# Moving low parts of weights and of g to GpSimd in the first tiles, under a new written order of all engines

## The chip, the cores and the metric

One core of a Trainium2 chip runs the whole program: TensorE (PE) multiplies, VectorE (DVE), ScalarE (ACT) and GpSimd (POOL) do the elementwise work, and SyncE (SP) issues every transfer between HBM and SBUF. The metric is the device time of one execution in microseconds, the median of several runs. Before the change it was 848.84 us in three runs (847.57 to 848.84).

## The reference

A sliding-window attention (window 64, 8 batches of 8 heads, 576 tokens, head size 64) is followed by a feed-forward layer on the 4608 x 512 result:

```python
scores = scale * np.matmul(q, k.transpose(0, 1, 3, 2))
mask = (rel >= 0) & (rel < window)           # rel = query position - key position
attn = exp(scores - max) / (sum + 1e-09)     # masked scores are -1e9
x = matmul(attn, v)                          # then tokens x (heads * head size)
h = x @ w_in                                 # 512 -> 2048
g = np.maximum(h, 0.0) ** 2
out = g @ w_out                              # 2048 -> 512
```

All inputs and outputs are float32.

## The kernel before, in words

**Tiles.** The 4608 tokens are 12 tiles of 384. Attention is done in sections of four pairs (a block of 64 queries, a group of heads), three sections to a tile: sections 0 to 2 make x of tile 0, 3 to 5 that of tile 1, 6 to 8 that of tile 2. The hidden size 2048 is 16 slices of 128, so a tile takes 16 steps, each a first product (12 matmuls, line 404) and a second one (9 matmuls, line 446).

**High and low parts.** A float32 operand of a product is split into a rounded high part and the rest, the low part; each product is made of three (high by high, high by low, low by high). The low part is one subtraction: line 132 for a weight slice (128 x 1024), line 423 for g (128 x 384), line 315 for x. A weight arrives as raw words and is first put together by two `tensor_scalar` (lines 120 and 121) and two `scalar_tensor_tensor` (lines 123 and 125) on VectorE, after ScalarE made its magnitude (line 118); ScalarE then writes the high part (line 129). Only two such weights can be under way, because the tile `a` has two halves. g is the square (line 416 on ScalarE, 418 otherwise) of the positive part (line 413).

**The order.** The work up to the first two steps of tile 2 stands in a string of tokens in the order in which each engine is to take its own: a letter, a number, and where there is a choice a last letter for the engine (d VectorE, a ScalarE, p GpSimd). The tokens that matter here:

| token | work | engine before |
|---|---|---|
| L, N, v, w, q, B | loads of q and k for tiles 0 and 1, of v, of a weight slice, of q and k of a later batch; a store of a finished slice | SP queue |
| T, U / t, u | transposes of q and k / their copies out of PSUM | PE / DVE or ACT |
| S, o, s, z, y, e f, k, R, m | scores of a section; copy, mask, maximum, scale, exponentials, sum, reciprocal, division | PE, ACT, DVE, DVE, POOL, ACT, POOL, DVE, POOL |
| X x V H Q | transposed weights, masking, product with v; high and low part of x | PE, DVE, PE, ACT, DVE |
| a b c d h l | the weight slice: lines 118, 120 and 121, 123, 125, 129, 132 | ACT, DVE, DVE, DVE, ACT, DVE |
| M, O | first and second product of a step | PE |
| r p g G | positive part, square, high part, low part of g | ACT, ACT (8 of 34 on DVE), ACT, DVE |
| D, Z, W, K | turn of a later batch, output copy, output store, matmuls with no result | DVE, ACT, SP, PE |

Each engine and the SP queue take their tokens strictly in this order; an instruction that waits holds all behind it. M0 to M4 are tile 0 with slices 0 to 4, M5 to M9 tile 1 with the same slices, then tile 1 runs ahead of tile 0 with slices 5 to 15: M22 is the first step that uses slice 15, the last one to be prepared. Behind the string a planner (lines 640 to 708) orders all later work; it is the same before and after.

**What VectorE does up to M22.** Through l15: the preparation of 16 weight slices (b, c, d, l), 21 low parts of g, one division, 5 copies, and of each of six sections the mask, maximum, reciprocal, x and Q; one H and two turns. GpSimd has only y, k and m of the sections up to there.

Of the kernel before, what the change touches and what calls it, by code (L numbers as in the profile page):

```python
# [8 lines left out]
F32 = mybir.dt.float32  # L9
# [3 lines left out]
ALU = mybir.AluOpType  # L13
# [16 lines left out]
def window_attention_relu2_ffn(ctx: ExitStack, tc: tile.TileContext, q, k, v, w_in, w_out, out):  # L30
# [74 lines left out]
        sp.dma_start(raw[:, 1], wo_v[:, f, :])  # L105


    def weight(op, f):
        if op == "a":
            wa[f] = a_t[:, f % 2].bitcast(I32)  # L110
        a = wa[f]
        if op in "acd":
            words = wraw[f].rearrange("p n (e w) -> p w (n e)", w=2)
            lower, upper = words[:, 0, :], words[:, 1, :]
        else:
            av = a.bitcast(F32).rearrange("p (n e) -> p n e", n=2)
        if op == "a":
            act.activation(a.bitcast(F32), upper.bitcast(F32), AF.Abs, scale=2.0 ** -80)
        elif op == "b":
            dve.tensor_scalar(a.bitcast(F32), a.bitcast(F32), 1.875 * 2.0 ** -64, 2.0 ** -95, ALU.min, ALU.max)  # L120
            dve.tensor_scalar(a, a, 4, 1, ALU.logical_shift_left, ALU.logical_shift_right)
        elif op == "c":
            dve.scalar_tensor_tensor(a, lower, 29, a, ALU.logical_shift_right, ALU.bitwise_or)  # L123
        elif op == "d":
            dve.scalar_tensor_tensor(a, upper, -0x80000000, a, ALU.bitwise_and, ALU.bitwise_or)  # L125
            wraw.pop(f)
        elif op == "h":
            wparts[f] = wpool.tile([P, 2, 2, DM], F32R, name="w")
            act.copy(wparts[f][:, :, 0], av)
        else:  # L130
            w = wparts[f]
            dve.tensor_tensor(w[:, :, 1], av, w[:, :, 0].bitcast(F32), ALU.subtract)  # L132
# [277 lines left out]
    def evac(op, n, eng=None):  # L410
        if op == "r":
            rg[n] = r_t[:, n % 2]
            act.activation(by_half(rg[n]), ordered(hs.pop(n)), AF.Relu)  # L413
        elif op == "p":
            if eng == "a":
                act.activation(rg[n], rg[n], AF.Square)
            else:
                dve.tensor_tensor(rg[n], rg[n], rg[n], ALU.mult)
        elif op == "g":
            gs[n] = (ghi_t[:, n % 3], glo_t[:, n % 2])  # L420
            act.copy(gs[n][0], rg[n])  # L421
        else:
            dve.tensor_tensor(gs[n][1], rg.pop(n), gs[n][0].bitcast(F32), ALU.subtract)  # L423

# [11 lines left out]
    hs, rg, gs = {}, {}, {}  # L436
# [43 lines left out]
    while n1 < NF:  # L480
# [18 lines left out]
        b12 O13 r14 p14a d11 g14 B4 M15 G14 h11 c12 O14 r15 l11 p15a g15 d12 a13 B5 M16 G15 h12 b13 O15 r16 l12
        p16a g16 c13 a14 B6 M17 G16 b14 O16 r17 p17a d13 g17 B7 M18 G17 h13 c14 O17 r18 l13 p18a g18 d14 a15 B8  # L500
        M19 G18 h14 b15 O18 r19 l14 p19a g19 c15 B9 M20 G19 D0 O19 r20 p20a d15 q2 g20 M21 G20 h15 D1 O20 r21
        l15 p21a g21 q3 G21 M22 O21 r22 p22d g22 G22 M23 D2 O22 r23 p23d q4 g23 M24 G23 Z22 W22 O23 r24 p24d g24
        G24 S6 M25 o6a D3 q5 s6 O24 r25 z6 p25a y6 g25 f6 G25 S7 O25 e6 o7d s7 v9 k6 z7 M26 R6 y7 m6p f7 D4 X6
# [42 lines left out]
    with tc.manual_schedule(engines={E.PE, E.DVE, E.Activation, E.Pool, E.SP}):  # L546
        for token in order.split():
            op, eng = token[0], token[-1] if token[-1] in "dap" else None
            n = int(token[1:].rstrip("dap"))
            if op in "LN":  # L550
                load_first("LN".index(op), n)
            elif op == "v":
                load_v(*divmod(n, (NB + 1) // 2))
            elif op == "w":
                fetch_w(n)
            elif op == "q":
                load_qk(1 + n // NPAIR, n % NPAIR)
            elif op == "D":
                turn(1 + n // NPAIR, n % NPAIR)
            elif op in "TU":  # L560
                ps_f[op, n] = turn_first("TU".index(op), *divmod(n, 2))
            elif op in "tu":
                copy_first("tu".index(op), *divmod(n, 2), ps_f[op.upper(), n], copier(eng))
            elif op == "K":
                idle(n)
            elif op in "abcdhl":
                weight(op, n)
            elif op == "M":
                hs[n] = mm1(*steps[n], lambda kk, part, f=steps[n][1]: wparts[f][:, 0, part, kk * P:(kk + 1) * P])
            elif op in "rpgG":  # L570
                evac(op, n, eng)
            elif op == "B":
                keep(n)
            elif op in "ACEF":
                mix(op, n)
            elif op == "O":
                mm2(*steps[n], *gs.pop(n), lambda part, f=steps[n][1]: wparts[f][:, 1, part])
            elif op in "ZW":
                for tb in range(NTB):
                    put(op, steps[n][0], tb)  # L580
            else:
                section(op, n, eng)
# [513 lines left out]
```

## Time and profile before

| what | value |
|---|---|
| median of 3 runs | 848.84 us (847.57 to 848.84) |
| profiled execution | 847.38 us, its span 845.1 us |
| PE busy | 829.0 us, 98% |
| DVE busy | 590.5 us, 70% |
| ACT busy | 407.3 us, 48% |
| POOL busy | 184.9 us, 22% |
| mean granted PE clock | 0.998 |

The span runs from the first instruction to the last; the rest of the execution's time, 2.3 us, lies around it. The page's busy shares are means over stages with different limits. The page also shows the span in 40 slices of 21 us: in the first seven, DVE is at 5, 8, 9, 9, 9, 9 and 6 tenths, and POOL at 1, 2, 2, 0, 0, 0 and 3 tenths, while PE is at 7 tenths in the first slice, 8 in the second and 9 or more from the third on.

### The profile page before, as it was taken

How to read it: one execution, taken by the hardware profiler on the slowest of the kernel's cores; microseconds unless marked ns; L12 is line 12 of the kernel's file. 1: busy time of each engine (PE TensorE's matmuls, PEld its weight loads, DVE VectorE, ACT ScalarE, POOL GpSimd, SP SyncE). 2: the span in 40 equal slices, each digit the busy share in tenths (PEclk: the TensorE clock that was granted, in tenths of full speed). 3: DMA queues.
4: the chain of work that ended last, by engine and by line, in shares of the span. 5: the costliest groups of instructions: out<-in, count | busy, mean ns of one | idle time of the engine just before them, and what ended most of it. 6: DMA issues, size and time to landing. Idle time of an engine off the chain costs nothing.

```text
span 845.1 us, 17706 instructions
## 1 busy us (share of the span) xinstructions
PE 829.0 (98%) x6754; PEld 761.2 (90%) x6754; DVE 590.5 (70%) x889; ACT 407.3 (48%) x1127; POOL 184.9 (22%) x239
## 2 busy tenths in 40 slices
PE   7899999999999999999999999999999999999998
PEld 5788989899999999999999999999999999999997
DVE  5899996746767866767687765788755668544553
ACT  5887874646446555544442354453454424222221
POOL 1220003204557420311320121141112132010110
PEclk9999999999999999999999999999999999999999
DMA  9989956584688875999896797999785556686411
GB/s 230 231 257 346 306 239 130 86 171 126 153 210 251 214 170 119 305 245 238 169 319 225 179 217 161 285 224 271 212 237 157 188 194 182 236 259 212 136 66 74
DMA packets 273012, 173.92 MB, mean 206 GB/s; under 512 B 190497, under 2 KB 239649, under 8 KB 270881
## 3 DMA queue, kind: packets, MB, share of 16 engines
q1 hardware_dynamic: 272928, 172.80, 73.8%
q8 instruction: 53, 0.87, 0.5%
q14 instruction: 31, 0.25, 0.1%
HBM read 138.15 MB, written 34.60 MB: 204 GB/s over the span
## 4 chain that ended last, share of the span: by engine, by line
PE 86%; SPq 5%; DVE 3%; DMA 3%; issue 2%; ACT 1%; POOL 0%; DVEq 0%; ACTq 0%; POOLq 0%
PE banks L993 29%; PE banks L912 26%; PE banks L446 11%; PE banks L404 11%; PE banks L235 3%; PE banks L298 3%; DMA w<-in_moe_w_out_dram 2%; PE banks L276 2%; SPq L147 1%; SPq L185 1%; SPq L157 1%; DVE a L123 1%; DVE a L125 1%; SPq L104 1%; DVE g L423 1%
## 5 line engine op out<-in xcount | busy, mean ns | idle before, releaser
L993 PE MATMUL banks<-w 128*128 128x512 f32 x1152 | 257.5, 380 | 0.0
L993 PEld LDWEIGHTS banks<-w 128*128 128x128 f32 x1152 | 215.7, 189 | 28.4
L404 PE MATMUL banks<-x,w 128*128 128x384 f32 x768 | 137.1, 328 | 1.9 <-ACT r L413 1.4
L446 PE MATMUL banks<-w,g 128*128 128x512 f32 x576 | 136.1, 382 | 0.2
L404 PEld LDWEIGHTS banks<-x,w 128*128 128x128 f32 x768 | 126.6, 189 | 6.1 <-ACT r L413 3.3
L912 PE MATMUL banks<-x,w 128*128 128x384 f32 x768 | 130.3, 326 | 0.0
L938 POOL TENSOR_TENSOR g<-g 128x384 f32<-128x384 f32 x64 | 59.5, 934 | 323.1 <-ACT g L949 308.2
L912 PEld LDWEIGHTS banks<-x,w 128*128 128x128 f32 x768 | 125.6, 189 | 0.0
L446 PEld LDWEIGHTS banks<-w,g 128*128 128x128 f32 x576 | 106.2, 189 | 14.4 <-DVE g L423 1.2
L263 ACT ACTIVATE sel<-sel,nm 128x64 f32<-128x64 f32 x272 | 90.8, 336 | 25.9 <-DVE nm L257 22.8
L912 PE MATMUL banks<-w 128*128 128x384 f32 x576 | 100.7, 329 | 0.0
L1001 DVE TENSOR_TENSOR w<-w,banks 128x512 f32<-128x512 f32 x72 | 49.5, 687 | 69.9 <-PE banks L993 69.9
L912 PEld LDWEIGHTS banks<-w 128*128 128x128 f32 x576 | 93.8, 189 | 1.9
L983 ACT CAST w<-w 128x512 fp32r<-128x512 f32 x48 | 29.8, 620 | 72.9 <-PE banks L993 72.9
L413 ACT ACTIVATE r<-banks 128x384 f32<-128x384 f32 x64 | 31.5, 492 | 66.8 <-PE banks L404 64.6
L983 ACT CAST w<-g 128x512 fp32r<-128x512 f32 x48 | 29.7, 621 | 62.2 <-PE banks L993 58.2
L272 POOL TENSOR_TENSOR sel<-sel,nm 128x512 f32<-128x512 f32 x33 | 36.1, 1095 | 107.3 <-ACT g L949 51.7
L263 ACT ACTIVATION_READ_ACCUMULATOR sel<-sel,nm 128x1 f32 x272 | 51.2, 188 | 0.0
L423 DVE TENSOR_TENSOR g<-r,g 128x384 fp32r<-128x384 f32 x64 | 37.6, 588 | 18.0 <-ACT g L421 9.7
L535 POOL TENSOR_TENSOR a<-w 128x256 f32<-128x256 f32 x28 | 24.9, 906 | 105.3 <-DVE w L132 79.6
L280 DVE TENSOR_TENSOR pt<-banks,masks 128x1024 f32<-128x1024 f32 x33 | 40.3, 1220 | 10.9 <-PE banks L276 10.9
L926 DVE TENSOR_TENSOR w<-banks,r 128x384 f32<-128x384 f32 x64 | 38.5, 601 | 13.3 <-PE banks L912 13.0
(103 smaller groups left out, 990.0 us busy)
## 6 DMA issues: line engine op xcount, KB each, us to landing
w<-mixed SPq DMA_DIRECT2D x128, 256.0 KB, 5.1
w<-kept SPq DMA_DIRECT2D x64, 512.0 KB, 7.2
w<-kept SPq DMA_DIRECT2D x96, 256.0 KB, 5.9
kept<-w SPq DMA_DIRECT2D x16, 1024.0 KB, 7.5
vt<-in_v_dram SPq DMA_DIRECT2D x144, 64.0 KB, 2.9
w<-in_moe_w_in_dram SPq DMA_DIRECT2D x16, 512.0 KB, 7.5
w<-in_moe_w_out_dram SPq DMA_DIRECT2D x16, 512.0 KB, 8.4
raw<-in_q_dram SPq DMA_DIRECT2D x112, 72.0 KB, 3.4
```

Of the source, the lines that this page charges most:

```text
L263: act.activation(sels[i][:, w, hd], sels[i][:, w, hd], AF.Exp, bias=nms[i][:, n], scale=SCALE, accum_out=sums[i][:, n])
L272: (dve if eng == "d" else pool).tensor_tensor(p, p, rs[i][:, :, None].broadcast_to([P, SW * 2, QB]), ALU.mult)
L280: dve.tensor_tensor(pts[i].rearrange("p (w n) q -> p w n q", n=2), ps_t[i][:, :, None, :].broadcast_to([P, SW, 2, P]), masks.rearrange("p ...
L404: pe.matmul(h_ps, lhsT=weights(kk, part), rhs=in_turn(x[xx][:, kk // 2, kk % 2]), start=n == 0, stop=n == 3 * NK - 1)
L423: dve.tensor_tensor(gs[n][1], rg.pop(n), gs[n][0].bitcast(F32), ALU.subtract)
L446: pe.matmul(acc(t, tb), lhsT=gg[:, ts], rhs=in_turn(weights(part)), start=f == 0 and n == 0, stop=f == NF - 1 and n == 2)
L912: pe.matmul(ps[:, :TT], lhsT=w[:, part, kk * P:(kk + 1) * P], rhs=in_turn(x[:, xx, kk]), start=n < 4 and m == 0, stop=m == 5, skip_group_c ...
L926: plan("dve", 0.6, lambda: dve.tensor_tensor(to(), ps, other(), ALU.add), [kps, ko], keys, 0, after)
L938: plan("pool", 0.95, lambda: pool.tensor_tensor(x(), x(), x(), ALU.mult), [], keys)
L983: plan("act", 0.62, lambda: act.copy(high(c), src()), g_keys, [kh], 0, freed("hi") if new else [])
L993: pe.matmul(ps, lhsT=gg[:, m // 2, m % 2], rhs=in_turn(wo_slot(w[m])[:, part]), start=m == 0 and n == 0, stop=m == 3 and n == 2)
L1001: plan("dve", 0.72, lambda: dve.tensor_tensor(by_half(parts(tb)), by_half(parts(tb)), ordered(ps), ALU.add), [key], [kp])
```

## The change

Three helper calls can now put their instruction on GpSimd, and the whole string of tokens is written anew, to the second step of tile 2. In the new string

- ten of the sixteen low parts of weights are GpSimd's (l0 to l3, l7, l8, l10 to l13); six stay with VectorE (4, 5, 6, 9, 14, 15);
- 23 of the 34 low parts of g are GpSimd's, 14 of the 34 squares too (16 stay with ScalarE, 4 with VectorE; before 26 and 8);
- of the copies t, VectorE has two and ScalarE eight (before five each); of the first six H, VectorE has three (0, 4, 5; before 5 alone); five y and six k move from GpSimd to VectorE; m0 moves from VectorE to GpSimd, m6 and m7 the other way;
- the loads stand in another order: q0 and q1 (eight transfers each) come early, weights 11, 9, 14 and 15 out of their turn, the stores B are strewn between them.

```diff
-    def weight(op, f):
+    def weight(op, f, eng=None):
...
             w = wparts[f]
-            dve.tensor_tensor(w[:, :, 1], av, w[:, :, 0].bitcast(F32), ALU.subtract)
+            (pool if eng == "p" else dve).tensor_tensor(w[:, :, 1], av, w[:, :, 0].bitcast(F32), ALU.subtract)
...
-                dve.tensor_tensor(rg[n], rg[n], rg[n], ALU.mult)
+                (pool if eng == "p" else dve).tensor_tensor(rg[n], rg[n], rg[n], ALU.mult)
...
-            dve.tensor_tensor(gs[n][1], rg.pop(n), gs[n][0].bitcast(F32), ALU.subtract)
+            (pool if eng == "p" else dve).tensor_tensor(gs[n][1], rg.pop(n), gs[n][0].bitcast(F32), ALU.subtract)
...
     order = """
-        L0 L1 w0 L2 T0 v0 T1 t0a t1d S0 w1 T2 o0a T3 K5 t2d v1 s0 t3d a0 z0 S1 L3 y0 b0 f0 N0 T4 K3 c0 o1a L4
...
-        h7 c8 O8 r9 l7 p9a g9 d8 a9 M10 G9 h8 b9 O9 r10 l8 p10a g10 c9 a10 B0 M11 G10 b10 O10 r11 p11a d9 g11 B1
...
+        L0 T1 T0 t0d L1 w0 t1a K3 S0 L2 o0a s0 z0 y0d T2 t2d T3 t3a w1 K11 S1 a0 L3 v0 b0 c0 f0 o1a s1 z1 y1d T4
+        t4a e0 k0d R0 K2 T5 t5a K4 S2 d0 a1 b1 m0p X0 x0 e1 o2a s2 z2 T6 t6a f1 K2 T7 t7a V0 k1p R1 S3 h0 c1 v1
+        y2p f2 H0d Q0 N0 U0 d1 m1p X1 u0a e2 k2d R2 x1 l0p o3a s3 z3 m2p L4 T8 t8a h1 K7 T9 w2 t9a X2 x2 V1 a2
+        H1a Q1 N1 U2 b2 u2a U1 c2 y3p f3 v2 l1p V2 w3 u1a S4 U3 H2a Q2 d2 e3 k3p R3 o4a s4 z4 y4d a3 m3p b3 w4
+        M0 X3 u3a S5 x3 h2 l2p v5 r0 c3 p0p f4 e4 k4p M1 R4 r1 o5a s5 v3 V3 g0 d3 H3a Q3 p1a g1 M2 a4 z5 G0p O0
+        b4 h3 m4p X4 x4 c4 d4 G1p r2 O1 w5 q0 p2a y5p l3p g2 G2p e5 f5 k5p v4 v6 h4 V4 H4d w6 M3 r3 O2 w8 R5 Q4
...
+        l8p a10 b10 c10 h9 l9d O9 G11p M12 O10 r12 p12p M13 r13 g12 O11 a11 D1 M14 w15 p13a g13 G13p d10 h10
...
-                weight(op, n)
+                weight(op, n, eng)
```

**GpSimd's queue around the first products.** Before, it holds only the sections' small steps up to the division of section 5:

```order
L272 TENSOR_TENSOR sel_79<-sel_79,nm_81 128x512
L266 TENSOR_SCALAR nm_81<-nm_81 128x8
L272 TENSOR_TENSOR w_111<-w_111,nm_81 128x512
L257 TENSOR_SCALAR nm_81<-nm_81 128x8
L266 TENSOR_SCALAR nm_81<-nm_81 128x8
```

Now, from the division of section 1 on:

```order
L272 TENSOR_TENSOR sel_79<-sel_79,nm_81 128x512
L132 TENSOR_TENSOR w_324<-a_84,w_324 128x2x512
L272 TENSOR_TENSOR w_111<-w_111,nm_81 128x512
L257 TENSOR_SCALAR nm_81<-nm_81 128x8
L132 TENSOR_TENSOR w_374<-a_84,w_374 128x2x512
L266 TENSOR_SCALAR nm_81<-nm_81 128x8
L272 TENSOR_TENSOR w_111<-w_111,nm_81 128x512
L132 TENSOR_TENSOR w_550<-a_84,w_550 128x2x512
L418 TENSOR_TENSOR r_82<-r_82 128x384
```

The divisions (line 272) of sections 2 and 3 now stand behind the low parts of weights 0 and 1 (line 132), and behind them come the low part of weight 2 and the first square (line 418).

**VectorE's queue in the middle of the weights** (`a_84` is the tile of two weights, the numbered `w` a raw slice or a finished one, `g_83` and `r_82` the tiles of g). Before, every slice takes its two `tensor_scalar`, lines 123 and 125, and a low part:

```order
L120 TENSOR_SCALAR a_84<-a_84 128x1024
L121 TENSOR_SCALAR a_84<-a_84 128x1024
L132 TENSOR_TENSOR w_1023<-a_84,w_1023 128x2x512
L123 SCALAR_TENSOR_TENSOR a_84<-w_727,a_84 128x1024
L423 TENSOR_TENSOR g_83<-r_82,g_83 128x384
```

Now two slices follow one another with no low part of a weight and one of g:

```order
L123 SCALAR_TENSOR_TENSOR a_84<-w_750,a_84 128x1024
L125 SCALAR_TENSOR_TENSOR a_84<-w_750,a_84 128x1024
L120 TENSOR_SCALAR a_84<-a_84 128x1024
L121 TENSOR_SCALAR a_84<-a_84 128x1024
L123 SCALAR_TENSOR_TENSOR a_84<-w_898,a_84 128x1024
L125 SCALAR_TENSOR_TENSOR a_84<-w_898,a_84 128x1024
L423 TENSOR_TENSOR g_83<-r_82,g_83 128x384
```

**GpSimd's queue at the same place** had nothing between the division of section 5 and the planner's first work; now it has

```order
L132 TENSOR_TENSOR w_949<-a_84,w_949 128x2x512
L423 TENSOR_TENSOR g_83<-r_82,g_83 128x384
L418 TENSOR_TENSOR r_82<-r_82 128x384
L423 TENSOR_TENSOR g_83<-r_82,g_83 128x384
L132 TENSOR_TENSOR w_1010<-a_84,w_1010 128x2x512
L423 TENSOR_TENSOR g_83<-r_82,g_83 128x384
```

These are l7, the low part of g of step 8, the square of step 10, the low part of g of step 9, l8 and the low part of g of step 11.

More of the change, by code (lines that the diff above doesn't have):

```diff
@@ L499, in window_attention_relu2_ffn @@
[L499 to L503, printed above, removed]
@@ new lines, in window_attention_relu2_ffn @@
+        O14 M17 a13 d12 h12 G15d O15 B8 b13 r17 p17a B7 c13 q3 d13 g17 p16p l12p g16 G16d a14 h13 M18 r18 p18a
+        G17p O17 g18 l13p M19 B5 a15 B9 b14 c14 d14 b15 r19 h14 l14d p19p O16 g19 M20 G19d G18p O18 r20 c15 d15
+        p20a g20 h15 M21 l15d O19 r21 M22 p21p q2 D2 G20p O20 r22 p22a g22 M23 g21 G21p r23 B3 O21 p23a g23 B1
+        G22p M24 r24 p24p g24 O22 Z22 M25 G23d r25 O23 M26 v8 D3 G24p O24 q4 r26 S6 p25p o6a s6 M27 v10 g25 z6
+        y6d G25p S7 o7d O25 p26a q5 D5 q7 r27 M28 g26 G26p O26 f6 e6 s7 z7 y7d f7 D4 r28 M29 p27d e7 g27 S8 G27p
```

19 lines of the change are left out of this document (7 added, 12 removed).

## The prediction

> **What bounds the kernel now.** I first read the busy time by stage: the stretch up to the first product, the one up to about M6, the one up to M22, and the rest of the written order. Columns are the stretch, its length, then the busy time of PE, weight loads, DVE, ACT and POOL, the granted clock, the DMA share and GB/s.
>
> ```profile
> 9.80:39.80 30.00, 25.22 (x406) 21.58 (x405) 27.64 (x41) 24.43 (x86) 6.46 (x12) 0.94 0.99 225
> 39.80:66.80 27.00, 25.11 (x263) 21.94 (x261) 26.57 (x33) 21.72 (x57) 4.80 (x6) 1.00 0.89 274
> 66.80:132.00 65.20, 64.95 (x346) 59.99 (x347) 63.63 (x70) 50.22 (x70) 0.01 (x1) 1.00 0.81 278
> 132.00:187.70 55.70, 55.13 (x517) 49.78 (x516) 33.50 (x51) 28.57 (x100) 13.82 (x24) 1.00 0.66 127
> ```
>
> VectorE is busy for 117.8 of the 122.2 us up to M22, and from 66.8 on PE is full too: both run without a gap, so whichever loses time there moves the end. Behind M22 PE is full alone (55.13 of 55.70), and the page shows it at 9 tenths or more in all slices but the first two. What M22 loses or gains therefore arrives at the end of the kernel: nothing later has room to take it back, and at most 0.6 us can be won in the last stretch.
>
> Second, the timelines of VectorE and PE at the borders of these stretches:
>
> ```profile
> 9.86 0.69 DVE L202 COPY qk<-banks 128x512 f32<-128x512 f32 x1 [2.06 <-PE banks L196]
> 12.38 0.68 DVE L120 TENSOR_SCALAR a<-a 128x1024 f32<-128x1024 f32 x1
> ...
> 38.33 0.69 DVE L315 TENSOR_TENSOR x<-banks,x 128x512 fp32r<-128x512 f32 x1
> ...
> 60.17 1.23 DVE L132 TENSOR_TENSOR w<-a,w 128x1024 fp32r<-128x1024 f32 x1
> 61.31 0.69 DVE L315 TENSOR_TENSOR x<-banks,x 128x512 fp32r<-128x512 f32 x1
> ...
> 130.73 1.18 DVE L132 TENSOR_TENSOR w<-a,w 128x1024 fp32r<-128x1024 f32 x1
> ```
>
> ```profile
> 39.85 2.20 PE L404 MATMUL banks<-x,w 128*128 128x384 f32 x12
> ...
> 130.03 2.11 PE L446 MATMUL banks<-w,g 128*128 128x512 f32 x9
> 131.97 2.11 PE L404 MATMUL banks<-x,w 128*128 128x384 f32 x12
> ```
>
> VectorE works from 9.86. Q2 (38.33, line 315) ends at 39.02 and M0 follows at 39.85. The last low part of a weight, l15, ends at 131.91, and M22, the first step with that slice, starts at 131.97. So there is no slack at M22: the time at which VectorE is through its list is the time of M22. An instruction begins 0.09 before the one ahead of it ends (61.31 against 60.17 + 1.23); I take 0.08 off each duration below. A second product is 1.94 (130.03 to 131.97).
>
> **Do the two engines work beside one another?** This decides the case, and the trace has it. Third, timelines of GpSimd and VectorE where both work, with the usual durations (minimum, median, maximum in ns) of two of the lines:
>
> ```profile
> 51.36 1.05 POOL L272 TENSOR_TENSOR sel<-sel,nm 128x512 f32<-128x512 f32 x1 [0.39 <-DVE nm L269]
> 51.69 1.80 DVE L132 TENSOR_TENSOR w<-a,w 128x1024 fp32r<-128x1024 f32 x1
> ...
> 43.13 1.33 DVE L125 SCALAR_TENSOR_TENSOR a<-w,a 128x1024 int32<-128x1024 int32 x1
> 43.27 1.27 POOL L266 TENSOR_SCALAR nm<-nm 128x8 f32<-128x8 f32 x1 [2.95 <-ACT sel L263]
> ...
> 417.89 1.83 POOL L864 TENSOR_TENSOR w<-a 128x768 f32<-128x768 f32 x1 [9.57 <-ACT a L313]
> 418.49 1.25 DVE L257 TENSOR_SCALAR nm<-nm 128x8 f32<-128x8 f32 x1
> ...
> 419.79 1.83 POOL L864 TENSOR_TENSOR w<-a,w 128x768 f32<-128x768 f32 x1
> 420.30 0.56 DVE L926 TENSOR_TENSOR w<-banks,r 128x384 f32<-128x384 f32 x1
> ...
> L132 DVE TENSOR_TENSOR w<-a,w x16: 1181/1218/1803, 18.4 to 130.7; 128x1024 fp32r<-128x1024 f32 x16
> ...
> L266 POOL TENSOR_SCALAR nm<-nm x10: 238/241/1270, 17.0 to 174.3; 128x8 f32<-128x8 f32 x10
> ```
>
> The low part of a weight, usually 1.22, took 1.80 and ended 1.08 after GpSimd's division (51.36 + 1.05 = 52.41): it stood still until GpSimd was through. The other way round, GpSimd's little addition, usually 0.24, took 1.27 and ended at 44.54, just behind VectorE's line 125 (44.46). VectorE's tiny scale at 418.49 ended at 419.74, with GpSimd's subtraction (419.72). But line 926, whose first operand lies in PSUM, ran its 0.56 inside a GpSimd subtraction. So GpSimd and VectorE take turns, for whole instructions, where VectorE works on SBUF alone (lines 120, 121, 123, 125, 132, 418, 423 and the tiny steps); beside its instructions with a PSUM operand GpSimd is free. I count transposes and reductions, too, as free.
>
> **The change, part by part: VectorE's list up to l15.** Groups of the trace up to M22 (busy us, mean ns):
>
> ```profile
> L125 DVE SCALAR_TENSOR_TENSOR a<-w,a 128x1024 int32<-128x1024 int32 x16 | 23.0, 1442 | 0.0
> L123 DVE SCALAR_TENSOR_TENSOR a<-w,a 128x1024 int32<-128x1024 int32 x16 | 22.2, 1392 | 0.0
> L132 DVE TENSOR_TENSOR w<-a,w 128x1024 fp32r<-128x1024 f32 x16 | 20.0, 1253 | 1.1 <-ACT w L129 1.0
> L423 DVE TENSOR_TENSOR g<-r,g 128x384 fp32r<-128x384 f32 x22 | 12.5, 567 | 0.0
> L120 DVE TENSOR_SCALAR a<-a 128x1024 f32<-128x1024 f32 x16 | 11.3, 708 | 1.0 <-ACT a L118 1.0
> L121 DVE TENSOR_SCALAR a<-a 128x1024 int32<-128x1024 int32 x16 | 11.1, 694 | 0.6
> ...
> L202 DVE COPY qk<-banks 128x512 f32<-128x512 f32 x4 | 2.7, 677 | 8.3 <-PE banks L196 8.3
> ```
>
> Removed: ten l of 1.25 - 0.08 = 1.17 (11.7 us), 13 G of 0.49 (6.4), and one division and three copies t, taken at 0.6 each by the copy's row (2.4; one of the copies is shorter). Added: two squares, priced as the low part of the same size (1.0), two H at a copy's price (1.2), five tiny y and k at 0.1 (0.5). Net 17.8 us less: 117.8 becomes 100.0.
>
> Of these 100.0, the lines that take turns with GpSimd are the four weight lines (67.6), six l (7.5), eight G (4.5), two squares (1.1) and the tiny ones (0.8): 81.5, less 0.08 for each of 85 instructions, 74.7. Free are 25.3.
>
> **GpSimd's list up to the same place**, through G18, which O18 before M21 needs. Prices from the whole span (minimum, median, maximum ns):
>
> ```profile
> L539 POOL TENSOR_TENSOR a<-a x56: 446/459/849, 135.0 to 301.6; 128x128 f32<-128x128 f32 x56
> ...
> L864 POOL TENSOR_TENSOR w<-a x3: 1822/1829/1839, 417.9 to 680.4; 128x768 f32<-128x768 f32 x3
> ...
> L938 POOL TENSOR_TENSOR g<-g x64: 824/829/1771, 338.7 to 818.4; 128x384 f32<-128x384 f32 x64
> ...
> L272 POOL TENSOR_TENSOR sel<-sel,nm x33: 1043/1046/1312, 23.6 to 669.0; 128x512 f32<-128x512 f32 x33
> ```
>
> No subtraction of 384 or 1024 columns on GpSimd is in the trace. The line through 128 columns (0.459) and 768 (1.829) gives 2.14 ns a column: 1.01 us for a G, and beyond its end 2.38 for an l (bounds: not under 1.83; in proportion to 768 columns 2.44). Ten l 23.8, twelve G 12.1, nine squares at 0.83 7.5, six divisions at 1.05 6.3, seven y and k at 0.24 1.7: 51.4 us, almost all in turns with VectorE. Each moved instruction holds VectorE up for about twice what it took there (2.38 for 1.25, 1.01 for 0.57).
>
> [...]
>
> **The sum at M22.** Least: every free us of VectorE lies beside GpSimd and nobody waits for anything else. From the first line 120 (12.38, hardly moved): 12.38 + 74.7 + 51.4 = 138.5. Most: none of it overlaps and VectorE's gaps of before (122.2 - 117.8 = 4.4) stay: 9.86 + 100.0 + 4.4 + 51.4 = 165.7. I take two thirds of the free 25.3 as covered (16.9), because GpSimd's queue nearly always has something while the sections run, and let the gaps be filled: 9.86 + 100.0 + 51.4 - 16.9 = 144.4. Against 131.97 that is 12.4 us later, with 6.5 and 33.7 as the ends. Besides, only 20 second products stand ahead of M22 now, before 21: 1.9 us of work is still to do. Together +14.3; the ends +8.4 and +35.6. Lines 123 and 125 may be quicker among more pauses: they took 1.21 at best, and 16 times 0.18 and 0.23 less would be 6.6, which brings the low end to +1.8.
>
> I cost the other edits at nothing. ScalarE loses ten squares and gains three copies; its 50.2 busy of 65.2 us covers that. Late next is the second product, which waits for G, itself behind an l in GpSimd's queue; and each a waits for the l two slices back, since `a` has two halves. All that lies inside the +14.3 as long as GpSimd and VectorE keep one another busy. The profiled execution took 847.38, the median is 1.5 higher. 847.4 + 14.3 + 1.5 = **863 us**. Its own range, from +1.8 to one third covered (+14.3 + 8.4): 851 to 872.
>
> **Rivals.**
>
> *GpSimd is a free hand after all* (not slower): the turns cost little and VectorE's list alone counts. Up to Q2 it is 4.4 us shorter (two l, three copies and the division go, an H and five tiny steps come, one R and one s move behind), so M0 comes 4.4 earlier, and the 1.9 us for which PE was idle between 39.8 and 66.8 go too: 849 - 6.3, about 842. For it speaks that VectorE is the fullest engine and POOL doing 0.01 us from 66.8 to 132; against it every pair quoted above. 13%.
>
> *Nearly in series* (slower still): the waits in a chain r, p, g, G with two steps on GpSimd, behind an l of 2.4 that waits for ScalarE, leave both engines idle in turn; then the sum goes to its upper end, +25 to +35.6: 879 as its likeliest. 11%.
>
> *A load comes late.* q0's eight transfers now stand ahead of the v of block 8 and weights 6 and 8:
>
> ```profile
> 40.29 0.50 SPq L104 DMA_DIRECT2D w<-in_moe_w_in_dram  x1
> ...
> 76.59 0.43 SPq L147 DMA_DIRECT2D raw<-in_q_dram  x1
> ...
> 87.27 0.50 SPq L147 DMA_DIRECT2D raw<-in_q_dram  x1
> ```
>
> Eight such issues took 10.7 us (76.59 to 87.27); weight 6, issued at 40.29 before (its first transfer), would be asked for some 11 us later or more, and b6 now stands ahead of Q5, for which M5 waits. What remains after the wait for GpSimd may be 4 us: 867. 10%.
>
> *It changes nothing:* the turns eat just what the shorter list gives, and M22 stays where it is, 849. The least sum already lies 6.5 above it. 5%.
>
> **How the numbers follow.** Forecast 61%, series 11%, load 10%, free hand 13%, nothing 5%. Faster by over 0.2% is 13%, within 0.2% (the runs before differ by 0.15%, so less can't be told) 5%, slower 82%. The range goes from 847 to 875: it leaves out the free hand and the upper half of the series, some 19%.
>
> **What would show it.** Right: on GpSimd, line 132 near 2.4 with none of its own waits, and on VectorE lines 120 to 125 and 423 stretched by one to two us wherever GpSimd works; M0 between 35 and 40, M22 at 140 or later, PE with gaps of one to three us between 80 and 145 that end on G of GpSimd or on VectorE; behind M22 the same stages as before, shifted. Wrong: lines 132 on GpSimd well under 2 us, VectorE's instructions unstretched beside them, PE full from M0 on, or M22 before 132.

## The result, and the profile after

The changed kernel takes 877.91 us (median of 4 runs, 877.12 to 879.46) where the kernel before took 848.84 (four runs by then, 847.57 to 850.64): a ratio of 1.0343 (95% interval 1.0319 to 1.0367), slower by 29 us. The prediction was 863 with a range of 847 to 875: the sign was right, but of the 29 us it had forecast 14. The profiled execution took 879.46 with a span of 877.7.

The busy time by stage of the changed kernel, cut at the end of l15 (columns as in the prediction: stretch, length, busy PE, weight loads, DVE, ACT and POOL, granted clock, DMA share, GB/s), and the last rows of VectorE and PE around that place:

```profile
66.80:152.32 85.52, 72.39 (x359) 62.38 (x359) 80.00 (x64) 44.95 (x64) 40.12 (x22) 0.98 0.75 221
9.86:152.32 142.46, 118.83 (x1004) 102.07 (x1002) 130.04 (x124) 87.62 (x201) 71.46 (x44) 0.96 0.79 218
```

```profile
148.46 1.52 DVE L125 SCALAR_TENSOR_TENSOR a<-w,a 128x1024 int32<-128x1024 int32 x1
151.09 1.23 DVE L132 TENSOR_TENSOR w<-a,w 128x1024 fp32r<-128x1024 f32 x1 [1.11 <-ACT w L129]
```

```profile
134.92 1.78 PE L446 MATMUL banks<-w,g 128*128 128x512 f32 x7 [1.46 <-POOL g L423]
...
151.50 0.59 PE L404 MATMUL banks<-x,w 128*128 128x384 f32 x2 [0.86 <-ACT r L413]
152.37 1.89 PE L404 MATMUL banks<-x,w 128*128 128x384 f32 x10 [0.28 <-DVE w L132]
...
157.04 3.05 PE L446 MATMUL banks<-w,g 128*128 128x512 f32 x7 [2.35 <-POOL g L423]
```

l15 ends at 152.32 (151.09 + 1.23), before at 131.91: 20.4 us later. M22 still waits for exactly that, so the mark by which the prediction reckoned was the right one. VectorE was busy for 130.04 of 142.46 us and idle for 12.4; before, idle for 4.3 (122.05 less 117.75). PE, full from 66.8 on before, now works 72.39 of 85.52 us there.

VectorE's groups up to 155 us and GpSimd's up to 190 (busy us, mean ns of one, idle time before them and its releaser):

```profile
L123 DVE SCALAR_TENSOR_TENSOR a<-w,a 128x1024 int32<-128x1024 int32 x16 | 29.4, 1837 | 0.4
L125 DVE SCALAR_TENSOR_TENSOR a<-w,a 128x1024 int32<-128x1024 int32 x16 | 27.0, 1685 | 0.3
L121 DVE TENSOR_SCALAR a<-a 128x1024 int32<-128x1024 int32 x16 | 18.6, 1164 | 0.6
L120 DVE TENSOR_SCALAR a<-a 128x1024 f32<-128x1024 f32 x16 | 14.5, 906 | 3.7 <-ACT a L118 3.6
```

```profile
L132 POOL TENSOR_TENSOR w<-a,w 128x1024 fp32r<-128x1024 f32 x10 | 27.1, 2706 | 17.3 <-ACT w L129 17.3
L423 POOL TENSOR_TENSOR g<-r,g 128x384 fp32r<-128x384 f32 x19 | 25.7, 1355 | 29.0 <-ACT g L421 28.3 <-PE banks L446 0.6
L418 POOL TENSOR_TENSOR r<-r 128x384 f32<-128x384 f32 x13 | 16.3, 1256 | 15.9 <-ACT r L413 14.1 <-DMA w<-in_moe_w_in_dram 1.8
```

The four weight lines sum to 89.5 us, 67.6 before, in the same 64 instructions. A pair of timelines (GpSimd above, VectorE below) shows how that comes about:

```profile
129.94 2.87 POOL L132 TENSOR_TENSOR w<-a,w 128x1024 fp32r<-128x1024 f32 x1 [3.79 <-ACT w L129]
132.77 2.09 POOL L423 TENSOR_TENSOR g<-r,g 128x384 fp32r<-128x384 f32 x1
```

```profile
129.88 0.70 DVE L121 TENSOR_SCALAR a<-a 128x1024 int32<-128x1024 int32 x1
130.61 3.39 DVE L123 SCALAR_TENSOR_TENSOR a<-w,a 128x1024 int32<-128x1024 int32 x1
```

GpSimd's low part starts beside line 121 and is through at 132.81; line 123, ready at 130.61, ends at 134.00, 1.19 behind it; and GpSimd's low part of g, 1.0 when alone, takes 2.09, as line 123 has its turn first.

Behind M22 there is a loss that the prediction did not have. The SP queue, ScalarE and PE of the changed kernel near 220 us:

```profile
218.11 2.67 SPq L457 DMA_DIRECT2D out_dram<-x  x3
```

```profile
217.82 0.51 ACT L421 CAST g<-r 128x384 fp32r<-128x384 f32 x1 [0.39 <-DVE r L418]
223.56 0.59 ACT L313 CAST x<-banks 128x512 fp32r<-128x512 f32 x1 [5.23 <-DMA out_dram<-x]
```

```profile
222.31 2.11 PE L446 MATMUL banks<-w,g 128*128 128x512 f32 x9
228.23 3.43 PE L404 MATMUL banks<-x,w 128*128 128x384 f32 x12 [3.82 <-ACT r L413]
```

The first high part of x of section 9 goes into the tile that holds the output of tile 0, and waits until that is stored. The store (W31) is issued at 218.11, because the new order writes Z31 and W31 behind g33, g32 and G32; then ScalarE stands still for 5.23 us, PE for 3.82, and the next product takes 3.43 in place of 2.11.

### The profile page after: what moved, and what is told of

Same layout as the page of the kernel before. It is cut to its first block, busy times and chain, and to the rows that moved or that the text cites. A ratio compares the mean times of both kernels' runs of the same rounds, so it can differ in the third digit from the quotient of the medians.

```text
span 877.7 us, 17710 instructions
## 1 busy us (share of the span) xinstructions
PE 838.4 (96%) x6754; PEld 764.2 (87%) x6754; DVE 598.4 (68%) x863; ACT 398.4 (45%) x1118; POOL 253.5 (29%) x274
## 4 chain that ended last, share of the span: by engine, by line
PE 81%; DVE 5%; SPq 4%; DMA 4%; ACT 2%; issue 2%; POOL 1%; POOLq 0%; ACTq 0%; DVEq 0%
PE banks L993 28%; PE banks L912 25%; PE banks L446 10%; PE banks L404 9%; PE banks L235 3%; PE banks L298 3%; DMA w<-in_moe_w_out_dram 2%; DVE a L123 2%; PE banks L276 2%; SPq L147 1%; SPq L157 1%; SPq L185 1%; DVE a L121 1%; SPq L104 1%; DMA w<-in_k_dram 1%
## 5 line engine op out<-in xcount | busy, mean ns | idle before, releaser
L446 PE MATMUL banks<-w,g 128*128 128x512 f32 x576 | 141.5, 390 | 11.9 <-DVE g L423 5.9
L404 PE MATMUL banks<-x,w 128*128 128x384 f32 x768 | 141.0, 333 | 8.4 <-ACT r L413 7.3
L446 PEld LDWEIGHTS banks<-w,g 128*128 128x128 f32 x576 | 107.3, 192 | 29.1 <-POOL g L423 8.3
L912 PE MATMUL banks<-x,w 128*128 128x384 f32 x768 | 130.3, 326 | 0.0
L272 POOL TENSOR_TENSOR sel<-sel,nm 128x512 f32<-128x512 f32 x32 | 37.0, 1156 | 121.8 <-ACT g L949 51.4
L931 DVE SCALAR_TENSOR_TENSOR w<-w 128x384 f32<-128x384 f32 x64 | 46.8, 731 | 1.7
L984 DVE TENSOR_TENSOR w<-g,w 128x512 fp32r<-128x512 f32 x48 | 32.6, 684 | 16.7 <-ACT w L983 16.7
```

The lines of the kernel that those rows point to most:

```text
L272: (dve if eng == "d" else pool).tensor_tensor(p, p, rs[i][:, :, None].broadcast_to([P, SW * 2, QB]), ALU.mult)
L404: pe.matmul(h_ps, lhsT=weights(kk, part), rhs=in_turn(x[xx][:, kk // 2, kk % 2]), start=n == 0, stop=n == 3 * NK - 1)
L446: pe.matmul(acc(t, tb), lhsT=gg[:, ts], rhs=in_turn(weights(part)), start=f == 0 and n == 0, stop=f == NF - 1 and n == 2)
L912: pe.matmul(ps[:, :TT], lhsT=w[:, part, kk * P:(kk + 1) * P], rhs=in_turn(x[:, xx, kk]), start=n < 4 and m == 0, stop=m == 5, skip_group_c ...
L931: plan("dve", 0.57, lambda: dve.scalar_tensor_tensor(x(), x(), 0.0, x(), ALU.max, ALU.mult), [], keys)
```

## The experiments

Each run is compared with runs of the kernel before on the same chip (medians of 848.6 to 849.2). Theory A: GpSimd and VectorE take turns on SBUF. Theory B: the order itself loses time. Theory C: GpSimd's own slowness stands in the chain r, p, g, G.

**The order alone.** One line of the string, in which nothing but the engine letters change:

```diff
-        l8p a10 b10 c10 h9 l9d O9 G11p M12 O10 r12 p12p M13 r13 g12 O11 a11 D1 M14 w15 p13a g13 G13p d10 h10
+        l8 a10 b10 c10 h9 l9 O9 G11 M12 O10 r12 p12a M13 r13 g12 O11 a11 D1 M14 w15 p13a g13 G13 d10 h10
```

> Only the new written order: every l and G is back on VectorE, and the fourteen squares that went to GpSimd are back on ScalarE; nothing else differs from the changed kernel. Theory A (GpSimd and VectorE take turns on SBUF, and that is what costs up to M22): VectorE's ten l and 23 G come back (about 1.2 and 0.5 us each), nothing holds it up, lines 123 and 125 fall from 1.84 and 1.69 to about 1.4, M22 starts between 132 and 138, and what is left of the loss is the late store of the last output tile, about 6 us: 850 to 860. Theory B (the order itself loses: loads later, a long idle stretch K7, the chain r-p-g-G, the late store): M22 at 145 or later and 870 to 880, with lines 123 and 125 unstretched all the same.

879.36 us, ratio 1.0357 (1.0342 to 1.0373): as slow as the changed kernel, though its low parts of weights and of g are back on VectorE and its squares off GpSimd. The small moves of the new string are still in it (copies t, y, k, m, H, and two more squares on VectorE), and no run parts them from the order; "the order alone" means both. Theory A's number is refuted for this run, B's holds. VectorE's lines 123 and 125 are as short as before (1.39 us each), and it idles for 24.9 us (145.32 less 120.43); some of the rows at which it does:

```profile
9.86:155.18 145.32, 117.39 (x999) 102.45 (x998) 120.43 (x146) 92.38 (x211) 11.00 (x13) 0.95 0.78 214
```

```profile
109.67 0.69 DVE L120 TENSOR_SCALAR a<-a 128x1024 f32<-128x1024 f32 x1 [1.99 <-ACT a L118]
...
117.68 0.56 DVE L423 TENSOR_TENSOR g<-r,g 128x384 fp32r<-128x384 f32 x1 [2.15 <-ACT g L421]
...
153.95 1.23 DVE L132 TENSOR_TENSOR w<-a,w 128x1024 fp32r<-128x1024 f32 x1 [1.11 <-ACT w L129]
```

VectorE stands before the step that ScalarE is just making for it. In the new string h9 (ScalarE) and l9 (VectorE) are neighbours; in the old one VectorE has b11 to do between h10 and l10. VectorE's waits for such a step of a weight or of g come to 11.9 us; the others are waits for PE or ScalarE in the sections.

**The engines alone**, in the order of before:

```diff
-        h7 c8 O8 r9 l7 p9a g9 d8 a9 M10 G9 h8 b9 O9 r10 l8 p10a g10 c9 a10 B0 M11 G10 b10 O10 r11 p11a d9 g11 B1
+        h7 c8 O8 r9 l7p p9a g9 d8 a9 M10 G9p h8 b9 O9 r10 l8p p10p g10 c9 a10 B0 M11 G10 b10 O10 r11 p11a d9 g11 B1
```

> The written order of before, with the same ten l, 23 G and fourteen p on GpSimd as in the changed kernel. Theory A: M22 is late by 12 to 25 us as VectorE's lines 120 to 125 are stretched, nothing is added behind M22 (the store of the last output tile is early there): 861 to 874. Theory B: with the old order M22 stays within 3 us of 132: 847 to 853. Theory C (the low parts are slow on GpSimd and stand in the chain r-p-g-G, whether or not VectorE is held up): PE waits on G of GpSimd by 1 to 3 us at many second products, and lines 123 and 125 keep about 1.4 us: 860 to 875.

870.23 us, ratio 1.0253 (1.0238 to 1.0268), in theory A's range and outside B's; C's range holds it too, but lines 123 and 125 are at 1.84 and 1.83, which C denies. That does not rule C out as a part of it: of the 19.6 us by which l15 ends later, VectorE's busy time is 4.4 (turns, less what was taken off its list), and 15.3 are pauses. VectorE waits 4.3 us for a step of GpSimd itself, and ScalarE 16.2 for squares and 8.2 for low parts of weights on GpSimd.

**One kind at a time**, in the order of before: the ten l, the 23 G, or the fourteen p (each the same letters as above, of one kind).

> The order of before, only the ten l on GpSimd. Theory A: 24 to 27 us of GpSimd work stretch VectorE by 12 to 20 while 11.7 of its list go: M22 1 to 10 us later, 850 to 860. Theory C (slow low parts in the chain): an l of 2.4 to 2.7 us delays the products of its slice, PE waits on w of GpSimd; 853 to 862 with lines 123 and 125 near 1.4. With neither: 840 to 849.

> The order of before, only the 23 G on GpSimd. Theory A: some 13 G of 1.0 to 1.4 us before M22 take as much from VectorE as the 6.4 us that they free or a little more: 848 to 856. Theory C: G is the last step before a second product, so that its longer duration (1.0 to 1.4 for 0.57, and the way to another engine's queue) is waited for by PE nearly each time, 0.5 to 1.5 us each: 855 to 870.

> The order of before, only the fourteen p on GpSimd, nine or ten of them before M22. VectorE's list does not change at all. Theory A: ten squares of 0.83 us hold VectorE up by 4 to 8 us: 853 to 857. Theory C: a square on GpSimd is about as long as on ScalarE, so PE waits little: 849 to 851.

The l: 854.50 us, ratio 1.0069 (1.0043 to 1.0095). The G: 852.42, 1.0041 (1.0026 to 1.0056). The squares: 853.34, 1.0053 (1.0033 to 1.0073). VectorE's mean of lines 123 and 125, with l15's end in brackets: 1.82 and 1.83 (139.59), 1.66 and 1.56 (137.61), 1.51 and 1.42 (137.49). The squares tell most: they take nothing off VectorE, yet l15 is 5.6 us later; VectorE's busy time is 3.7 longer (121.42 for 117.75), and 1.9 are pauses. They are not free of the chain, though: ScalarE waits 12.5 us for them up to l15. C's range for the G is refuted; PE waits for G of GpSimd by 1.1 us in all there.

The three delays of l15, 7.7, 5.7 and 5.6, add up to 19.0, and all together it was 19.6; but that is luck. Of each, a part is there at M0 already (M0 at 40.48, 43.08 and 40.05, and at 40.99 with all three, for 39.85), and for the G, 3.2 us before any of them has gone to GpSimd. Behind M0 the delays are 7.1, 2.5 and 5.4, 14.9 in all, against 18.5; the medians add up to 12.6 against 21.6. So the three together cost more than apart. Of this, 3.7 us lie behind l15: there PE waits 1.99 us for a low part of g on GpSimd, and the matmuls that follow are slower (seven in 2.77 us for 1.78, twelve in 2.86 for 2.11), which happens in none of the three.

**The disputed cost by itself.** The kernel before, word for word, and twelve GpSimd subtractions that nobody needs:

```diff
+    def spare(n):
+        out = extra[:, :1024].rearrange("p (a b) -> p a b", a=4)
+        m = masks.rearrange("p n j q -> p (n j q)")[:, None].broadcast_to([P, 4, 256])
+        for _ in range(n):
+            pool.tensor_tensor(out, m, m, ALU.subtract)
```

> The kernel before, word for word, with twelve spare subtractions of 128x1024 on GpSimd behind m5 (from about 63 us on, where GpSimd is idle until 132): they read a constant and write into a buffer that nobody reads until later, and nobody waits for them. So neither order nor chain changes; only the two engines' nearness is measured. Theory A by whole turns: each holds VectorE up for its whole duration, 12 times 2.4 is 28 us less what falls beside reads of PSUM and transposes, M22 near 155, 868 to 876. Theory A by half (what VectorE's sum in the changed kernel shows: 30 us of stretch beside about 60 of added GpSimd work): 12 to 16 us, 860 to 866. Theories B and C (order and chain): within 2 us of 849, with lines 123 and 125 unstretched.

867.49 us, ratio 1.0218 (1.0199 to 1.0237). B and C cannot be the cause here: nothing of the program has changed but GpSimd's company. The number lies between the two ranges of theory A, 0.5 us under that of whole turns. GpSimd's row, VectorE's, and the same instructions once GpSimd is through:

```profile
54.98 29.52 POOL L518 TENSOR_TENSOR w<-masks 128x1024 f32<-128x1024 f32 x12
```

```profile
58.44 2.26 DVE L121 TENSOR_SCALAR a<-a 128x1024 int32<-128x1024 int32 x1
60.62 1.21 DVE L280 TENSOR_TENSOR w<-banks,masks 128x1024 f32<-128x1024 f32 x1
...
63.46 2.24 DVE L423 TENSOR_TENSOR g<-r,g 128x384 fp32r<-128x384 f32 x1
65.62 2.91 DVE L125 SCALAR_TENSOR_TENSOR a<-w,a 128x1024 int32<-128x1024 int32 x1
...
70.62 0.68 DVE L313 CAST x<-banks 128x512 fp32r<-128x512 f32 x1
71.22 2.31 DVE L132 TENSOR_TENSOR w<-a,w 128x1024 fp32r<-128x1024 f32 x1
...
96.64 0.69 DVE L121 TENSOR_SCALAR a<-a 128x1024 int32<-128x1024 int32 x1
97.25 0.55 DVE L423 TENSOR_TENSOR g<-r,g 128x384 fp32r<-128x384 f32 x1
```

A low part of g takes 2.24 beside GpSimd and 0.55 alone, line 121 2.26 and 0.69; lines 280 and 313, which read PSUM, keep their 1.2 and 0.68. l15 ends at 152.81 (151.63 + 1.18), 20.9 later. Of this, 2.6 us are there before the first spare instruction: M0 starts at 42.42 for 39.85, as PE waits longer for loads of q and k in this execution. The other 18.3, which is also the difference of the medians, are the price of 28.7 us of GpSimd work (12 times 2.39, with its own waits): each microsecond of GpSimd cost 0.64. The window up to there parts it:

```profile
9.86:152.81 142.95, 122.50 (x1011) 108.10 (x1010) 134.19 (x142) 96.52 (x212) 39.12 (x29) 0.93 0.77 226
```

VectorE's busy time grew by 16.4 (134.19 less 117.75), which is 0.57 of GpSimd's; the other 4.5 are pauses (8.8 for 4.3). About half of these lie ahead of M0 (4.6 idle up to 39.80, before 2.3); the largest behind it is a wait of 2.00 us for ScalarE, which had itself waited 1.72 for VectorE.

**The same with fills**, first into the same buffer, then into one that nobody waits for (`pool.memset(out, 0.0)`, 24 times, `out` being the probabilities' tile in the second run).

> As the run with twelve spare subtractions, but with 24 spare fills of 128x1024 with zero in their place: about as long on GpSimd (1.1 us each, 27 in all), but they read nothing. If any GpSimd work on SBUF holds VectorE up: VectorE's instructions beside them take 1.1 and more, M22 10 to 20 us later, 858 to 866. If it is two operands that are read: VectorE's instructions keep their usual durations and the time is 848 to 851. From the kernel with fills for low parts, where lines 120 and 121 stayed stretched (0.92 and 0.98) and 123 and 125 hardly (1.51, 1.50), something between, for lines 120 and 121 alone: 850 to 856.

> The kernel before with the 24 spare fills again, written into the buffer of section 5's probabilities behind V5, where nobody waits for them before about 150 us. If only lines 120 and 121 of VectorE are held up by fills (about 0.75 us each, some six to eight of them beside the fills): M22 4 to 6 us later, 852 to 856. If the 7 us of the first run came from the wait for the buffer: 849 to 851.

856.03 us (1.0089, 1.0067 to 1.0111), where ScalarE's h waited 2.7 us for the buffer, so that this run measures two things, and lies at the upper edge of what was given; and 852.54 (1.0038, 1.0025 to 1.0052) without that, as expected if fills hold up lines 120 and 121 alone. GpSimd's and VectorE's rows of the second run:

```profile
59.98 20.90 POOL L518 MEMSET pt<- 128x1024 f32 x19
```

```profile
62.08 0.54 DVE L423 TENSOR_TENSOR g<-r,g 128x384 fp32r<-128x384 f32 x1
...
63.28 1.23 DVE L132 TENSOR_TENSOR w<-a,w 128x1024 fp32r<-128x1024 f32 x1
...
66.59 1.40 DVE L121 TENSOR_SCALAR a<-a 128x1024 int32<-128x1024 int32 x1
...
70.80 2.67 DVE L123 SCALAR_TENSOR_TENSOR a<-w,a 128x1024 int32<-128x1024 int32 x2
```

Beside fills line 121 still doubles (1.40 for 0.69), but the two-operand lines 423, 132 and 123 (2.67 for two) are as when alone. So it depends on both sides: what GpSimd reads decides whether the two-operand instructions of VectorE wait; `tensor_scalar` waits for either.

**Write-only low parts** in the changed kernel:

```diff
-            (pool if eng == "p" else dve).tensor_tensor(w[:, :, 1], av, w[:, :, 0].bitcast(F32), ALU.subtract)
+            if eng == "p":
+                for _ in range(3):
+                    pool.memset(w[:, :, 1].bitcast(F32), 0.0)
```

> The changed kernel, with each low part that GpSimd makes (ten l, 23 G) replaced by three fills of the same region with zero: GpSimd is busy about as long and later steps wait for it in the same way, but it reads nothing. Those low parts are left out of the computation. Theory A, if it is the reading of two operands that holds VectorE up: lines 123 and 125 near 1.4 us, M22 at 135 to 142, 860 to 868 in all with the late store. Theory A, if any GpSimd work on SBUF does it, and theory C (GpSimd's own duration in the chain): 873 to 881; these two are told apart by lines 123 and 125, stretched to 1.7 and more by the first, near 1.4 by the second.

870.71 us, ratio 1.0250 (1.0232 to 1.0268), between the two ranges given, 7.2 under the changed kernel. Up to M22 the first theory has it: l15 ends at 140.79 (135 to 142 was given), 11.5 earlier than in the changed kernel, and lines 123 and 125 are nearly short again:

```profile
L123 DVE SCALAR_TENSOR_TENSOR a<-w,a 128x1024 int32<-128x1024 int32 x16 | 24.1, 1507 | 0.4
L125 DVE SCALAR_TENSOR_TENSOR a<-w,a 128x1024 int32<-128x1024 int32 x16 | 24.0, 1501 | 0.3
```

VectorE's busy time is 15.2 us shorter than in the changed kernel (114.84), its pauses 3.7 longer. GpSimd works as long (73.2 and 71.5 us up to l15), so its mere duration is not what M22 pays for. One thing differs beside the reading: the fills do not wait for ScalarE's high parts, and ScalarE's line 118 no longer waits for low parts on GpSimd (6.0 us in the changed kernel). What is missing at the end went behind M22, where O20 waits 4.1 us for GpSimd and the late store costs PE 4.6.

**The store early**, in the changed kernel:

```diff
-        H8d Q8 G31p D6 y9p f9 e9 M32 r32 p32a k9d R9 O31 M33 r33 m9p p33d g33 g32 X9 v11 B2 G32d Z31 W31 x9 G33p"""
+        H8d Q8 G31p D6 y9p f9 e9 M32 r32 p32a k9d R9 O31 Z31 W31 M33 r33 m9p p33d g33 g32 X9 v11 B2 G32d x9 G33p"""
```

> The changed kernel, with the last output tile's sum and store (Z31, W31) written right behind its last product O31 and no longer behind g33, g32 and G32. If section 9's first step waits for that store because its tile is the one being stored: the wait of 5.2 us on the output goes, PE's wait of 3.8 us in that place and the lower granted clock behind it too, 870 to 874. If that wait lay beside other work: 876 to 880.

874.08 us (872.37 to 875.36), ratio to before 1.0297 (1.0281 to 1.0313): 3.8 less than the changed kernel, at the upper edge of the first range given. The store is issued at 211.31, and the waits on the output and of PE behind it are gone:

```profile
211.31 1.42 SPq L457 DMA_DIRECT2D out_dram<-x  x3
```

```profile
223.64 2.11 PE L404 MATMUL banks<-x,w 128*128 128x384 f32 x12
```

**The copies alone**, in the kernel before (`t3d t6d t9d` become `t3a t6a t9a`).

> The kernel before, with the three copies t3, t6 and t9 of the first blocks on ScalarE, as in the changed kernel. Nothing of this is on GpSimd. VectorE loses about 2 us of its list ahead of M0; if its list sets M0 and M22, 846 to 848. If ScalarE, which is busy for 24.4 of the first 30 us, becomes the one that is waited for: 849 to 852.

849.01 us, ratio 1.0006 (0.9993 to 1.0019): no change. VectorE's list is 0.8 shorter up to l15 (116.94 for 117.75), ScalarE 25.83 busy in the first 30 us, and M0 starts at 40.02 for 39.85. These 0.8 us, handed to ScalarE, won nothing.

**Why order and engines don't add.** The order alone costs 31 us, the engines alone 22, both 29. The new order was cut at Q5: up to there its tokens, behind it the rest in the order of before. Once with the engines of before, once with those of the changed kernel. The junction in the first:

```diff
+        y5p l3 g2 G2 e5 f5 k5p v4 v6 h4 V4 H4d w6 M3 r3 O2 w8 R5 Q4 l4 m5p X5 M4 x5 V5 p3a a6 B0 g3 G3 O3 b6 H5d a5 Q5
+        w7 v7 v8 w9 w10 w11 w12 w13 w14 w15 b5 r4 M5 p4a c5 g4 q1 c6 r5 M6 p5a G4 g5 d6 O4 r6 d5 h6 G5 p6a M7 h5 g6 l5
...
```

> Order alone, but the new order only as far as Q5 (some 66 us), and behind it the rest in the order of before; all l and G on VectorE as before, the last output tile's store early as before. Order theory 1 (behind Q5 the new order writes dependent steps next to one another on two engines: h and l of one slice, a and b, g and G; VectorE idles 14.3 us there against 1.6 before): VectorE's idle time behind 66.8 falls to 2 to 4, M22 near 141 to 146, 857 to 863. Order theory 2 (all of it comes from the late loads and the head, and only shows later): M22 stays at 150 or more, 868 to 874.

> The new order as far as Q5, the rest in the order of before (as in the run of 858.2), now with the engines of the changed kernel. If the moves to GpSimd seem free in the changed kernel because the new order leaves VectorE pauses behind Q5 anyway (24.9 us idle in the order alone, 12.4 in the changed kernel): here, where only 2.6 us of pause are left behind 66.8, the moves show most of their price, 868 to 878. If it is the new order that makes good use of GpSimd, wherever it stands: 856 to 862.

858.20 us (1.0111, 1.0096 to 1.0126) and 867.95 (1.0219, 1.0188 to 1.0250). The first is as order theory 1 says: with the old order behind Q5 the loss falls from 31 to 9. (The loads of weights 7 and 9 to 15 move forward with it; with the order alone, ScalarE's line 118 waits for no load up to l15, so these are not the reason.) The second stands at the lower edge of its first reading: here the moves cost 9.8. Windows up to l15, in the order of before with the new engines, in the new order up to Q5 with the old engines, and with the new ones:

```profile
9.86:151.55 141.69, 119.41 (x1011) 103.09 (x1010) 122.11 (x118) 88.02 (x201) 70.66 (x50) 0.98 0.76 228
```

```profile
9.86:143.18 133.32, 119.31 (x1009) 105.82 (x1010) 119.64 (x145) 97.03 (x214) 11.79 (x13) 0.94 0.82 242
```

```profile
9.86:149.65 139.79, 117.42 (x1004) 101.57 (x1003) 129.47 (x121) 87.50 (x203) 74.98 (x46) 0.98 0.77 231
```

| order | engines before: time, l15's end, VectorE idle | engines after |
|---|---|---|
| before | 848.8, 131.91, 4.3 | 870.2, 151.55, 19.6 |
| new to Q5 | 858.2, 143.18, 13.7 | 868.0, 149.65, 10.3 |
| new | 879.4, 155.18, 24.9 | 877.9, 152.32, 12.4 |

The moves cost 21 us in an order with 4.3 us of pauses, 10 in one with 13.7, and nothing in one with 24.9. VectorE's time is its list, the turns of GpSimd, and its pauses. In the order of before the moves make VectorE 4.4 us busier and 15.3 more idle; in the new one 9.6 busier and 12.5 less idle (130.0 and 12.4 for 120.4 and 24.9). That the moves cost nothing there does not mean that the turns do: with write-only low parts l15 ended 11.5 us earlier in the same order. What the moves take off VectorE's list and out of its pauses, the turns take back. That the turns fill pauses which the order had made anyway is read from these columns, not shown by a run of its own. Which of the two is to blame for the 29 us can't be said of either alone: each would have cost over 20.

## Why the prediction was right or wrong

*M22 as the mark: right.* l15 still ends last, and M22 follows it.

*The turns: right in kind, somewhat too large.* The twelve spare subtractions show them by themselves, with the exceptions that the prediction named (lines 280 and 313 untouched). Its list of 100.0 us plus 34.5 of turns (51.4 less 16.9) made 134.5 busy for VectorE; it was 130.04, so by that list the turns came to 30.0. By the run of the order alone (120.43 less ten l and twelve G, 101 to 103) they came to 27 to 29. GpSimd's own instructions took 71.5 us in place of 51.4, for the most part because GpSimd waits its turn as well. On one point it was too coarse: it had every GpSimd instruction take turns with every SBUF line; the fills show that for the two-operand lines this holds only when GpSimd reads. The change moves only subtractions and products of two operands, so the sum didn't suffer.

Beside this, what the Trainium skill says (SBUF — State Buffer, section "Who interferes with whom"): VectorE instructions in a two-port mode (`tensor_scalar` can be) contend with GpSimd, and those with two SBUF inputs contend with a GpSimd instruction that reads SBUF, not with one that only writes it. The runs agree: line 423 took 2.24 us beside subtractions and 0.54 beside fills, line 121 2.26 and 1.40. No run shows in which mode line 121 worked.

*"And let the gaps be filled": the step that failed.* The prediction dropped VectorE's 4.4 us of pauses and put none in their place; there were 12.4. By its own sum: 9.86 + 130.04 + 12.4 = 152.3 in place of 144.4, 7.9 more, namely 12.4 of pauses less 4.5 of turns. What VectorE waited for in the changed kernel up to l15 (us in total, times, the longest):

```profile
DVE a L120 <- ACT a L118: 3.6, 3, 1.6
DVE pt L280 <- PE banks L276: 3.1, 1, 3.1
DVE sel L252 <- ACT sel L243: 2.8, 1, 2.8
...
```

(Of the 2.8, 2.0 lie ahead of 9.86.) The largest of these waits come from the new order and its loads, not from GpSimd's company. Ahead of the 3.1, PE waits for the load of a q (1.69) and does 3.35 us of matmuls with no result (K7), which the new order puts there. Of the 3.6, 3.05 follow on waits of ScalarE for loads, those of weights 6 and 7:

```profile
64.98 1.25 ACT L118 ACTIVATE a<-w 128x1024 f32<-128x1024 f32 x1 [2.90 <-DMA w<-in_moe_w_out_dram]
...
82.46 1.56 ACT L118 ACTIVATE a<-w 128x1024 f32<-128x1024 f32 x1 [1.66 <-DMA w<-in_moe_w_out_dram]
```

```profile
66.26 0.69 DVE L120 TENSOR_SCALAR a<-a 128x1024 f32<-128x1024 f32 x1 [1.60 <-ACT a L118]
...
84.06 0.69 DVE L120 TENSOR_SCALAR a<-a 128x1024 f32<-128x1024 f32 x1 [1.45 <-ACT a L118]
```

Weight 6 is asked for at 56.79 (before, at 40.29), behind the eight transfers of q0 and six of a v; weight 7 at 76.95, behind those of q1. The rest are waits of about 1 us and less for a step that ScalarE is just making. The two engines do not keep one another busy, as the prediction put it: the new order makes 24.9 us of pauses with no low part on GpSimd, and the runs with turns have pauses too (8.8 in the spare run, 10.3 to 19.6 in the three with the new engines). What the prediction read in the diff was what leaves VectorE's list, not how far a step stands from the one, or from the load, that it waits for.

*"I cost the other edits at nothing": wrong.* Behind M22 the late store costs 3.8 (877.91 less 874.08). Besides, O20's wait for a low part of g on GpSimd, 2.35, and 1.73 more for its seven matmuls and the next product (3.05 for 1.78, 2.57 for 2.11): 4.1. In GpSimd's queue that low part stands behind 2.80 us of line 535, which had waited 7.55 us for l15. "Nothing later has room to take it back" was right, but it had room to lose more.

The parts sum up in the profiled executions: 20.4 at M22, 1.9 for the second product fewer (as predicted), 4.1 at O20, and 5.6 at the store (3.82 of wait, 1.83 in two slower products), together 32.0 of the 32.6 us by which the spans differ. Between the medians the difference is 29.1, and the store's part 3.8.

*The rivals.* Nearly in series gave 879, the right time, but by waits in the chain that GpSimd makes; the order alone gives the same time with all of that chain on VectorE and ScalarE, so the number is luck. Such waits are there (ScalarE's line 118 waits 6.0 us for low parts on GpSimd), but of VectorE's pauses in the changed kernel only one of 0.35 follows right on them. The free hand is refuted by the spare run. The late load came as described, at weight 6 and again at weight 7, and stands behind 3.05 us of VectorE's pauses (4 was given); it is a part, not the whole, and with the order alone the time is the same without it. "Nothing" is refuted by the result.

*What was to show it.* Line 132 on GpSimd took 2.35 at least, the estimate being 2.38, but 2.71 on average, for GpSimd too waits its turn. Single instructions of VectorE are stretched by up to 2 us (the four weight lines by 0.2 to 0.5 on average), M0 is at 39.78, M22 past 140, PE's longest gaps end on G: as named. Same stages behind M22, only shifted: not so.

## What to carry to other kernels

In this kernel an instruction that reads SBUF was not taken off VectorE by giving it to GpSimd while VectorE worked on SBUF itself: each microsecond of GpSimd held VectorE up by 0.64, and a low part that took VectorE 1.17 took GpSimd 2.4. Test such a move with spare instructions that nobody waits for, before anything is reordered: one run gives the price, free of order and chain. Read it from the medians, or behind a place that both executions have passed: at M0 single executions already differed by up to 3 us. And price a rewritten order by the distance between dependent steps on two engines, and by where it puts the loads and the stores that free a buffer; here it cost as much as the engines did, and either alone would have been enough.

## What was not expected of the hardware

GpSimd's fills held up `tensor_scalar` on VectorE (line 121, 1.40 for 0.69) but none of the two-operand instructions beside them (line 423, 0.54). The other is the price of a short wait of PE: after the wait of 2.35 us at O20 seven matmuls took 3.05 us, in place of the 1.78 behind the wait of 1.46, and behind the one of 3.82 twelve of line 404 took 3.43 in place of 2.11, with a granted clock of 0.93 between 215 and 240:

```profile
215.00:240.00 25.00, 20.49 (x216) 18.22 (x215) 13.80 (x23) 11.14 (x35) 9.10 (x14) 0.93 0.54 120
```

It isn't the length of the wait alone: with the order alone, a wait of 2.63 us left the clock where it was.

```profile
100.14 1.78 PE L446 MATMUL banks<-w,g 128*128 128x512 f32 x7 [2.63 <-DVE g L423]
```

What else decides it, the runs leave open.
